# Attention scores on half the rows of TensorE, two heads in turn, and an instruction order ranked backward from the end

## The chip, the cores and the metric

The kernel runs on one core of a Trainium2 chip. A core has TensorE (PE in the profile; PEld is its weight loads), VectorE (DVE), ScalarE (ACT), GpSimd (POOL) and SyncE (SP), whose queue issues all of this kernel's DMAs. TensorE reads two operands of up to 128 rows from the on-chip memory and adds its products up in PSUM, which has eight banks of 512 columns. The metric is the device time of one launch in microseconds (us).

## What is computed

```python
scores = scale * np.matmul(q, k.transpose(0, 1, 3, 2))      # q, k, v: (4, 8, 576, 64)
thresh = np.max(scores, axis=-1, keepdims=True) - tau
scores = np.where(scores >= thresh, scores, -1000000000.0)
attn = np.exp(scores - np.max(scores, axis=-1, keepdims=True))
attn = attn / (np.sum(attn, axis=-1, keepdims=True) + 1e-09)
attn_out = np.matmul(attn, v)                               # -> x: (2304, 512)
x = (1 / (1 + np.exp(-(x @ w_gate))) * (x @ w_val)) @ w_out # first layer, d_ff 1536
out = (((x @ w1) * (x @ w2)) @ w3) @ w_out2                 # second layer, d_ff 1024
```

The inputs of the two layers come in double width and are turned into single width on the chip. Every product is made of three: an operand x is split into a high part and a low part (xh + xl), and high x low, low x high and high x high are added up in PSUM.

## The kernel before

**Attention.** The 4 batches of 8 heads are 16 pairs of heads. A pair's query and key are loaded (qm, km), turned on TensorE so that the 64 features of each of the two heads lie in rows (head 0 in rows 0 to 63, head 1 in 64 to 127), and split: xq and yq are the high and low parts of the scaled query, xk and yk those of the key. Each pair has nine slots: four blocks of 128 queries for each head, and one for the last 64 queries of both heads (qb holds them, with zeros in the other head's rows). A slot's scores (128 queries x 576 keys) are made by `s_mm` in two halves of 288 columns, into one of two PSUM tiles, `sbuf_[g % 2]`, for slot g (named ps_s). Then `s_max` on VectorE takes each row's maximum (L648), `s_exp` on ScalarE runs twice over the scores (L656, L657; the second writes e and the sum), `s_hi` and `s_lo` split e into two parts of half width (L668 or L666, L674), a DMA turns them (pt), and five slots later `pv` multiplies by the values (64-column matmuls into u). `x_norm`, `x_pe` and `x_act` normalise the pair's result and put it into XR (L732, L734).

**Two forms of the scores.** `ZP = 2 * NPAIR` makes the first eight pairs (pr < ZP) differ from the last eight. In the first eight, one head's query lies in qst[h] (named qa) and kst[h] (ka) with zeros in the other head's rows, so that a product over all 128 rows gives this head alone: three products, six matmuls a slot. In the last eight, `dup0` and `dup1` stack xq over yq and xk over xk by DMA, and `low0` and `low1` put yk over zeros (ylz): two products, four matmuls a slot, for ten DMAs a pair. Slots go through one head's four blocks, then the other's.

**Fillers.** Between slots, `fill` takes pieces of other work for TensorE: first `merge_gen` (w3 times w_out2, names ps, th, tl, woh, wol), then `l1_gen`, the first layer (ps_h, ps_o), three quarters of which lie beside the attention; its weights are cast on VectorE, ScalarE and GpSimd (w, t) and split (gh, vh, oh and gl, vl, ol). The last quarter, and the second layer (ps_ab, ps_y), come after the last pair.

**What sets the order.** Everything up to `cut`, the end of the attention, is put in order by the class `Plan`. It has a cost for each instruction, knows what must wait for what (`hard`: for the end of it; `soft`: for its begin only), and lays the instructions out engine by engine: of those ready, the one with the lowest rank goes next, and the rank is the place in the program. `pin` ties each engine's instructions to this order. What comes after `cut` is not planned.

Of the kernel before, what the change touches and what calls it, by code (L numbers as in the profile page):

```python
# [21 lines left out]
class Plan:  # L22
# [10 lines left out]
    SLACK = {"DMACopy": 3000.0, "DmaTransposeAnt": 1500.0}  # L33
    HOLD = 200.0

    def __init__(self, insts, cut, over, late=(), by=0):
# [137 lines left out]
    def time(self, n):  # L174
# [32 lines left out]
    def order(self):  # L207
# [100 lines left out]
def kernel(  # L308
# [22 lines left out]
    nc = tc.nc  # L331
# [15 lines left out]
    def mm(out_, lhsT, rhs, first, last):  # L347
        nc.tensor.matmul(out_, lhsT, rhs, start=first, stop=last)  # L348

# [41 lines left out]

    ZP = 2 * NPAIR
    qst = [[ap_.tile([P, NC * P], F32R, name=f"qa{h}_{i}") for i in range(2)] for h in range(2)]
    kst = [[ap_.tile([P, S], F32R, name=f"ka{h}_{i}") for i in range(2)] for h in range(2)]
# [3 lines left out]
    ylz = [ap_.tile([P, S], F32R, name=f"ylz_{h}") for h in range(2)]  # L398
    tails = ap_.tile([P, H, D], F32, name="tails")

    def attn_setup():
# [4 lines left out]
        for h in range(2):  # L406
            z = hsl[1 - h]
            nc.vector.tensor_copy(
                ylz[h][z].rearrange("p (a d) -> p a d", d=D),
                zf[z].rearrange("p (a d) -> p a d", a=1).to_broadcast([D, S // D, D]),  # L410
            )
        for h in range(2):
            z = hsl[1 - h]
            for t in (*qst[h], *(t[:, 0:NC * P] for t in kst[h])):
# [63 lines left out]
    def q_act(pr):  # L478
# [4 lines left out]
        nc.scalar.activation(xk[:, NM:S], pt[:, TL:2 * TL], AF.Copy)  # L483
        xq = ap_.tile([P, NM], F32R, tag="xq", name="xq", bufs=1)
        p.update(xq=xq, qb=qbd[pr % 2])
# [8 lines left out]
    def q_dve(pr):  # L494
# [6 lines left out]
        )  # L501
        yq = ap_.tile([P, NM], F32R, tag="yq", name="yq", bufs=1)
        p["yq"] = yq
# [10 lines left out]
        for sl in hsl:  # L514
# [3 lines left out]
            )  # L518

    def dup(pr, h):  # L520

        p = prep[pr]
        xq, yq, xk = (p[n].bitcast(F32) for n in ("xq", "yq", "xk"))
        if pr < ZP:
            return
        qa = qst[h][pr % 2]
        nc.sync.dma_start(qa[hsl[h]].bitcast(F32), xq[hsl[h]])
        nc.sync.dma_start(qa[hsl[1 - h]].bitcast(F32), yq[hsl[h]])
        ka = kst[h][pr % 2]
        for sl in hsl:  # L530
            nc.sync.dma_start(ka[sl].bitcast(F32), xk[hsl[h]])
        p.setdefault("qa", []).append(qa)
        p.setdefault("ka", []).append(ka)

    def low(pr, h):

        if pr < ZP:
            return
        nc.sync.dma_start(ylz[h][hsl[h]].bitcast(F32), prep[pr]["yk"][hsl[h]].bitcast(F32))

    def low0(pr):
        low(pr, 0)

    def low1(pr):
        low(pr, 1)

    def dup0(pr):
        dup(pr, 0)

    def dup1(pr):  # L550
        dup(pr, 1)

# [64 lines left out]

    def s_mm(g):
        pr, s = divmod(g, NSL)
        p = prep[pr]  # L620
        ps = sbuf_[g % 2][:, SO:SO + S]
        if s < 2 * NC:
            h, c = divmod(s, NC)
            cs = slice(c * P, (c + 1) * P)
            if pr < ZP:
                x, y = qst[h][pr % 2][:, cs], kst[h][pr % 2][:, cs]
                prods = [(x, p["xk"]), (y, p["xk"]), (x, p["yk"])]
            else:
                prods = [(p["qa"][h][:, cs], p["ka"][h]), (p["qa"][h][:, cs], ylz[h])]
        else:  # L630
            prods = [
                (p["qb"][:, 0, :], p["xk"]),
                (p["qb"][:, 1, :], p["xk"]),
                (p["qb"][:, 0, :], p["yk"]),
            ]
        for i, (a, r) in enumerate(prods):
            for j in range(2):
                mm(
                    ps[:, j * HS:(j + 1) * HS], a, r[:, j * HS:(j + 1) * HS],
                    i == 0, i == len(prods) - 1,  # L640
                )
        st[g] = {"ps": ps}

# [37 lines left out]
    def pv(g, g_at):  # L681
# [5 lines left out]
        if s < 2 * NC:  # L687
            h, c = divmod(s, NC)
            todo = [(h, p["u"][:, h, c, :])]
# [9 lines left out]
    def x_norm(pr):  # L699
# [436 lines left out]
    t_pe(0, 0)  # L1136
    for step in (q_pe, q_act, q_dve, k_pe, k_act, k_dve, dup0, low0, dup1, low1):
        step(0)
# [8 lines left out]
        3: ([k_act], [k_dve], [], [v_pe1], []),  # L1147
        4: ([], [v_scale], [dup0, low0, dup1, "k"], [], []),
# [3 lines left out]
        8: ([], [], [low1, "v"], [], []),  # L1152
    }
# [35 lines left out]
    for g in range(G + LAG + 3):  # L1189
# [313 lines left out]
```

## Time and profile before

| | |
|---|---|
| median of 3 runs | 1071.82 us (1071.23 to 1078.38) |
| the profiled execution | 1074.56 us, its span 1072.8 us |
| TensorE busy | 1004.5 us, 94% of the span |
| VectorE, ScalarE, GpSimd busy | 673.1, 663.7, 692.4 us |
| last of the attention into XR | 631.84 us |

The span is from the first to the last instruction; the 1.8 us beside it are not in the trace. A share of the whole span mixes stages with different limits, and TensorE's ends are modelled, so that its busy time says less than the distance from one matmul's start to the next one's.

### The profile page before, as it was taken

How to read it: one execution, taken by the hardware profiler on the slowest of the kernel's cores; microseconds unless marked ns; L12 is line 12 of the kernel's file. 1: busy time of each engine (PE TensorE's matmuls, PEld its weight loads, DVE VectorE, ACT ScalarE, POOL GpSimd, SP SyncE). 2: the span in 40 equal slices, each digit the busy share in tenths (PEclk: the TensorE clock that was granted, in tenths of full speed). 3: DMA queues.
4: the chain of work that ended last, by engine and by line, in shares of the span. 5: the costliest groups of instructions: out<-in, count | busy, mean ns of one | idle time of the engine just before them, and what ended most of it. 6: DMA issues, size and time to landing. Idle time of an engine off the chain costs nothing. (4 is left out here: it accounts for less than half of the span.)

```text
span 1072.8 us, 20181 instructions
## 1 busy us (share of the span) xinstructions
PE 1004.5 (94%) x7088; PEld 891.5 (83%) x7088; DVE 673.1 (63%) x1226; ACT 663.7 (62%) x1325; POOL 692.4 (65%) x587
## 2 busy tenths in 40 slices
PE   4599976899998999999999989999999999999997
PEld 3488865687887888888888879999999989989995
DVE  8896587777866655557554447776776725743741
ACT  6687699978879878879887664445432322422221
POOL 5966288899997777667766756767664723552530
PEclk9999969999999999999999999999999999999999
DMA  8899699999999999989987675767378619835822
GB/s 218 237 238 226 146 234 220 254 224 268 252 251 228 219 211 223 209 191 210 232 171 164 130 178 186 255 223 236 129 248 276 204 60 321 258 98 173 310 78 59
DMA packets 301844, 221.28 MB, mean 206 GB/s; under 512 B 221872, under 2 KB 250544, under 8 KB 301744
## 3 DMA queue, kind: packets, MB, share of 16 engines
q1 hardware_dynamic: 301744, 220.00, 80.9%
q8 instruction: 56, 0.92, 0.4%
q14 instruction: 44, 0.36, 0.1%
HBM read 133.17 MB, written 30.93 MB: 153 GB/s over the span
## 5 line engine op out<-in xcount | busy, mean ns | idle before, releaser
L674 POOL TENSOR_TENSOR h<-e,h 128x576 f16<-128x576 f32 x120 | 155.1, 1295 | 75.7 <-ACT h L668 43.0
L648 DVE TENSOR_SCALAR_CACHE_REDUCE e<-ps_s,tauc 128x576 f32<-128x576 f32 x144 | 117.1, 814 | 72.2 <-PE ps_s L348 31.9
L656 ACT ACTIVATE ps_s<-ps_s,nt 128x576 f32<-128x576 f32 x144 | 102.4, 712 | 50.0 <-DVE e L648 48.4
L657 ACT ACTIVATE e<-ps_s,ebias 128x576 f32<-128x576 f32 x144 | 106.5, 740 | 2.9 <-POOL vl L781 0.4
L348 PEld LDWEIGHTS <-pt 128*128 128x128 f16 x2240 | 76.7, 100 | 32.6 <-issue 23.1
L348 PE MATMUL ps_h<-xl,gh 128*128 128x512 f32 (+1 forms) x240 | 93.1, 388 | 3.9 <-POOL xl L781 2.8
L348 PE MATMUL ps_h<-xl,vh 128*128 128x512 f32 (+1 forms) x240 | 92.5, 385 | 0.0
L348 PE MATMUL ps_y<-wm,abh 128*128 128x512 f32 x288 | 91.4, 390 | 0.3 <-DVE wm L781 0.3
L348 PE MATMUL ps_o<-gvl,oh 128*128 128x512 f32 (+1 forms) x240 | 90.7, 378 | 0.0
L348 PE MATMUL ps_h<-xh,gh 128*128 128x512 f32 (+1 forms) x240 | 89.1, 371 | 0.0
L348 PE MATMUL ps_h<-xh,gl 128*128 128x512 f32 (+1 forms) x240 | 88.9, 371 | 0.0
L348 PE MATMUL ps_h<-xh,vh 128*128 128x512 f32 (+1 forms) x240 | 88.8, 370 | 0.0
L348 PE MATMUL ps_h<-xh,vl 128*128 128x512 f32 (+1 forms) x240 | 88.8, 370 | 0.0
L348 PE MATMUL ps_o<-gvh,ol 128*128 128x512 f32 (+1 forms) x240 | 88.5, 369 | 0.0
L348 PE MATMUL ps_o<-gvh,oh 128*128 128x512 f32 (+1 forms) x240 | 88.3, 369 | 0.0
L668 ACT ACTIVATE h<-e 128x576 f16<-128x576 f32 x126 | 86.0, 684 | 2.9 <-DMA pt<-h 1.5
L781 POOL TENSOR_TENSOR gl<-w,gh 128x512 fp32r<-128x512 f32 x42 | 55.0, 1310 | 49.3 <-ACT gh L780 48.7
L781 POOL TENSOR_TENSOR gvl<-gr,gvh 128x512 fp32r<-128x512 f32 (+1 forms) x48 | 60.3, 1256 | 10.2 <-ACT gvh L780 9.6
L780 ACT ACTIVATE abh<-r 128x384 fp32r<-128x384 f32 x48 | 24.2, 521 | 68.9 <-DVE r L1368 68.6
L781 POOL TENSOR_TENSOR ol<-w,oh 128x512 fp32r<-128x512 f32 x42 | 55.8, 1336 | 16.7 <-ACT oh L780 16.7
L781 POOL TENSOR_TENSOR vl<-w,vh 128x512 fp32r<-128x512 f32 x43 | 58.1, 1352 | 8.7 <-ACT vh L780 8.4
L348 PEld LDWEIGHTS ps_y<-wm,abh 128*128 128x128 f32 x288 | 54.0, 188 | 11.4 <-DVE wm L781 0.6
(208 smaller groups left out, 3021.0 us busy)
## 6 DMA issues: line engine op xcount, KB each, us to landing
wc<-sc_c SPq DMA_DIRECT2D x168, 256.0 KB, 3.4
w<-sc_w SPq DMA_DIRECT2D x35, 768.0 KB, 5.2
sc_c<-wc SPq DMA_DIRECT2D x56, 256.0 KB, 2.7
XR<-in_moe_w_out_dram SPq DMA_DIRECT2D x20, 512.0 KB, 4.9
sc_w<-w SPq DMA_DIRECT2D x11, 768.0 KB, 5.9
XR<-in_moe_w_dram SPq DMA_DIRECT2D x16, 512.0 KB, 4.7
raw<-in_moe_w_dram SPq DMA_DIRECT2D x16, 512.0 KB, 4.6
XR<-in_moe_w_gate_dram SPq DMA_DIRECT2D x12, 512.0 KB, 5.5
```

What stands on the lines that cost most here:

```text
L348: nc.tensor.matmul(out_, lhsT, rhs, start=first, stop=last)
L648: nc.vector.tensor_scalar(e, x["ps"], tauc, None, op0=ALU.add, op1=ALU.min, accum_out=nt)
L656: nc.scalar.activation(x["ps"], x["ps"], AF.Prelu, scale=-1.0, bias=x["nt"], alpha=STEEP)
L657: nc.scalar.activation(x["e"], x["ps"], AF.Exp, bias=ebias, accum_out=prep[pr]["sum"][:, s:s + 1])
L668: nc.scalar.activation(x["h16"][:, 0:S], x["e"], AF.Copy)
L674: eng.tensor_tensor(hb[:, S:2 * S], st[g]["e"], hb[:, 0:S], op=ALU.subtract)
L780: nc.scalar.activation(hi, x, AF.Copy)
L781: (lo_eng or nc.gpsimd).tensor_tensor(lo, x, hi.bitcast(F32), op=ALU.subtract)
```

## The change

The stacking DMAs and the zero-filled rows of the scores go (`ZP = 0 * NPAIR`; dup and low are gone, ylz too). Every pair's slots, but the ninth, take three products over the head's own 64 rows: head 0's operands lie in rows 0 to 63 of xq, yq, xk, yk, head 1's in rows 64 to 127. `s_mm` gets two slots at once, the two heads' slots of one block of queries, and writes their matmuls in turn, so that both PSUM tiles are filled together; slots now go block by block, head by head. xq and yq get two buffers each. The eight GpSimd copies of zeros into qst and kst stay.

`Plan` is told of each such row of matmuls (`beads`): within it a matmul waits only for the begin of the one ahead. It gets a cost for matmuls on 64 rows, and a new rank: `pin` runs `order` and `backward` twice, and `backward` lays the instructions out from the end, so that the rank becomes the order of the latest begins.

```diff
-    ZP = 2 * NPAIR
+    ZP = 0 * NPAIR
+    beads = []
...
-        xq = ap_.tile([P, NM], F32R, tag="xq", name="xq", bufs=1)
+        xq = ap_.tile([P, NM], F32R, tag="xq", name="xq", bufs=2)
...
-    def s_mm(g):
+    def s_mm(*gs):
+
+        todo = []
+        for g in gs:
+            pr, s = divmod(g, NSL)
+            p = prep[pr]
+            ps = sbuf_[g % 2][:, SO:SO + S]
+            c, h = divmod(s, 2)
+            cs = slice(c * P, (c + 1) * P)
...
+                sl = hsl[h]
+                xq, yq, xk, yk = p["xq"][sl, cs], p["yq"][sl, cs], p["xk"][sl], p["yk"][sl]
+            todo.append((ps, [(xq, xk), (yq, xk), (xq, yk)]))
+            st[g] = {"ps": ps}
+        row = []
+        for i in range(3):
+            for j in range(2):
+                js = slice(j * HS, (j + 1) * HS)
+                for ps, prods in reversed(todo):
+                    a, r = prods[i]
+                    mm(ps[:, js], a, r[:, js], i == 0, i == 2)
+                    row.append(len(nc.cur_bb.bb.instructions) - 1)
+        if len(gs) > 1:
+            beads.append(row)
...
+    def group(g):
+
         pr, s = divmod(g, NSL)
...
+        if pr < ZP or s == 2 * NC:
+            return [g]
+        return [] if s % 2 else [g, g + 1]
...
-    for step in (q_pe, q_act, q_dve, k_pe, k_act, k_dve, dup0, low0, dup1, low1):
+    for step in (q_pe, q_act, q_dve, k_pe, k_act, k_dve):
...
-            if g + 2 < G:
-                s_mm(g + 2)
             if g + 1 < G:
                 s_max(g + 1)
                 s_exp(g + 1)
+            if g + 2 < G and group(g + 2):
+                s_mm(*group(g + 2))
...
     def pin(self, tc):
+        for _ in range(self.ROUNDS):
+            self.order()
+            self.backward()
```

TensorE's order in pair 4 before: the two slots of a ps_s tile each, six matmuls a slot (x2 stands for the two halves), with other work between them.

```order
L348 MATMUL ps_s_91<-xk,qa_0_95 128x288 x2
L348 MATMUL ps_s_91<-xk,ka_0_99 128x288 x2
L348 MATMUL ps_s_91<-yk,qa_0_95 128x288 x2
L721 MATMUL ps_x<-ident,xn 128x128 x4
L348 MATMUL ps_h<-xl,gh 128x512
L348 MATMUL ps_h<-xh,gl 128x512
L348 MATMUL ps_h<-xh,gh 128x512
L348 MATMUL ps_s_92<-xk,qa_0_95 128x288 x2
L348 MATMUL ps_s_92<-xk,ka_0_99 128x288 x2
L348 MATMUL ps_s_92<-yk,qa_0_95 128x288 x2
```

After, in pair 4: one group, the two tiles in turn, with nothing between.

```order
L409 MATMUL ps_s_92<-xk,xq 128x288
L409 MATMUL ps_s_91<-xk,xq 128x288
L409 MATMUL ps_s_92<-xk,xq 128x288
L409 MATMUL ps_s_91<-xk,xq 128x288
L409 MATMUL ps_s_92<-xk,yq 128x288
L409 MATMUL ps_s_91<-xk,yq 128x288
L409 MATMUL ps_s_92<-xk,yq 128x288
L409 MATMUL ps_s_91<-xk,yq 128x288
L409 MATMUL ps_s_92<-yk,xq 128x288
L409 MATMUL ps_s_91<-yk,xq 128x288
L409 MATMUL ps_s_92<-yk,xq 128x288
L409 MATMUL ps_s_91<-yk,xq 128x288
```

The first of these now follows the last exponential of both tiles' earlier slots, where each tile's first matmul followed its own alone. In the last eight pairs TensorE's order before had four matmuls a slot, here between pieces of the first layer; in their place stands the same row of twelve a group.

```order
L348 MATMUL ps_h<-xh,vh 128x512
L348 MATMUL ps_s_92<-ka_0_97,qa_0_93 128x288 x2
L348 MATMUL ps_s_92<-ylz_106,qa_0_93 128x288 x2
L348 MATMUL ps_h<-xl,vh 128x512
```

ScalarE's order before, slots 58 and 59 (pair 6): the passes over the scores of the one tile and of the other, with other steps spread between.

```order
L656 ACTIVATE ps_s_91<-ps_s_91,nt 128x576
L657 ACTIVATE e,sum<-ps_s_91,ebias 128x576
L558 ACTIVATE xk<-ps_t 128x512
L780 ACTIVATE gh<-w 128x512
L668 ACTIVATE h_3598<-e 128x576
L767 ACTIVATE t_3625<-XR 128x512
L780 ACTIVATE gvh<-gr 128x512
L780 ACTIVATE vh<-w 128x512
L656 ACTIVATE ps_s_92<-ps_s_92,nt 128x576
L767 ACTIVATE t_3676<-XR 128x512
L657 ACTIVATE e,sum<-ps_s_92,ebias 128x576
```

After, the same slots, to the first pass of the next group.

```order
L689 ACTIVATE e,sum<-ps_s_91,ebias 128x576
L700 ACTIVATE h_3584<-e 128x576
L688 ACTIVATE ps_s_92<-ps_s_92,nt 128x576
L689 ACTIVATE e,sum<-ps_s_92,ebias 128x576
L812 ACTIVATE gvh<-gr 128x512
L1033 ACTIVATE th<-ps_h 128x512
L812 ACTIVATE gh<-w 128x512
L799 ACTIVATE t_3611<-XR 128x512
L700 ACTIVATE h_3675<-e 128x576
L614 ACTIVATE vb<-vs 128x128
L688 ACTIVATE ps_s_91<-ps_s_91,nt 128x576
```

The two slots' passes moved together, and six other steps now stand between the group's last and the next group's first.

## Rows read from the trace of the kernel before

**Rows 1.** Windows of L648, cut at pairs' first: busy us (count), clock, DMA share, GB/s.

```profile
59.80:100.90 41.10, 7.36 (x18) 1.00 1.08 232
...
321.20:632.00 310.80, 59.11 (x144) 0.99 0.93 198
```

**Rows 2.** Windows, the same cuts: busy us (count) of PE, PEld, DVE, ACT, POOL.

```profile
0.00:13.10 13.10, 5.13 (x20) 4.42 (x21) 10.09 (x22) 4.65 (x8) 6.11 (x18) 1.00 0.68 191
13.10:59.80 46.70, 26.45 (x150) 22.17 (x150) 41.40 (x78) 36.03 (x69) 39.98 (x33) 1.00 0.94 237
59.80:100.90 41.10, 40.76 (x339) 35.23 (x338) 32.52 (x65) 33.84 (x68) 25.24 (x23) 1.00 1.08 232
100.90:138.40 37.50, 34.02 (x340) 29.40 (x339) 19.26 (x42) 25.16 (x50) 12.02 (x10) 0.95 0.73 165
138.40:170.60 32.20, 21.94 (x218) 19.98 (x214) 26.61 (x54) 30.82 (x64) 28.56 (x25) 0.68 1.07 230
170.60:199.40 28.80, 22.51 (x238) 18.63 (x235) 20.41 (x46) 26.48 (x56) 25.07 (x21) 1.00 1.10 250
199.40:236.70 37.30, 33.62 (x251) 28.14 (x250) 27.84 (x56) 31.44 (x64) 33.94 (x29) 0.95 1.05 229
236.70:278.00 41.30, 40.11 (x328) 33.22 (x326) 32.25 (x63) 32.12 (x63) 38.55 (x32) 1.00 1.06 274
278.00:321.20 43.20, 43.20 (x339) 36.35 (x336) 29.57 (x61) 36.26 (x71) 41.14 (x34) 1.00 1.07 239
321.20:632.00 310.80, 305.29 (x2554) 251.65 (x2552) 174.17 (x353) 253.95 (x509) 217.17 (x174) 0.99 0.93 198
```

**Rows 3.** The chain that ended last, in order of time: start, length, what.

```profile
631.84 0.31 ACT XR L734
...
1033.03 32.65 PE ps_y L348 x144
```

**Rows 4.** TensorE's timeline in pair 7: start and length in us.

```profile
300.73 0.43 PE L348 MATMUL ps_s<-xk,qa 128*128 128x288 f32 x2
...
301.52 0.23 PE L348 MATMUL ps_s<-identb,vm 128*128 128x128 bf16 x1
...
301.79 0.47 PE L348 MATMUL ps_h<-xl,vh 128*128 128x512 f32 x1
302.11 0.39 PE L348 MATMUL ps_h<-xh,vl 128*128 128x512 f32 x1
302.34 0.40 PE L348 MATMUL ps_h<-xh,vh 128*128 128x512 f32 x1
```

**Rows 5.** TensorE's timeline in pair 12.

```profile
482.71 0.42 PE L348 MATMUL ps_s<-ka,qa 128*128 128x288 f32 x2
...
483.24 0.39 PE L348 MATMUL ps_h<-xl,vh 128*128 128x512 f32 x1
```

**Rows 6.** Groups by line and shape: busy us, mean ns, idle before them.

```profile
L348 PEld LDWEIGHTS <-pt 128*128 128x128 f16 x2240 | 76.7, 100 | 32.6 <-issue 23.1 <-DMA pt<-h 6.8 <-DMA km<-in_k_dram 0.5
L648 DVE TENSOR_SCALAR_CACHE_REDUCE e<-ps_s,tauc 128x576 f32<-128x576 f32 x144 | 117.1, 814 | 72.2 <-PE ps_s L348 31.9 <-PE ps_s L725 8.4 <-PE ps_s L473 8.1
L656 ACT ACTIVATE ps_s<-ps_s,nt 128x576 f32<-128x576 f32 x144 | 102.4, 712 | 50.0 <-DVE e L648 48.4
L657 ACT ACTIVATE e<-ps_s,ebias 128x576 f32<-128x576 f32 x144 | 106.5, 740 | 2.9 <-POOL vl L781 0.4
L348 PE MATMUL ps_s<-ylz,qa 128*128 128x288 f32 x128 | 27.7, 299 | 0.0
L488 ACT ACTIVATE qa<-ps_t,zq 64x512 fp32r<-64x512 f32 x16 | 10.9, 680 | 0.3
L490 ACT ACTIVATE xq<-ps_t,zq 128x512 fp32r<-128x512 f32 x8 | 5.6, 703 | 0.0
```

**Rows 7.** Waits in pairs 3 to 7 (138.4 to 321.2 us): total, times, longest.

```profile
ACT ps_s L656 <- DVE e L648: 13.4, 15, 1.8
...
PE ps_s L348 <- ACT e L657: 8.3, 7, 1.8
```

More of the change, by code (lines that the diff above doesn't have):

```diff
@@ L34, with __init__ @@
     HOLD = 200.0
-    def __init__(self, insts, cut, over, late=(), by=0):
+    ROUNDS = 2
+    def __init__(self, insts, cut, over, late=(), by=0, beads=()):
         self.later = [i for i in insts[cut:] if i.opcode in self.OPS]
@@ L48, in __init__ @@
         self.edges(over)
+        at = {i.name: n for n, i in enumerate(self.x)}
+        for row in beads:
+            row = [at[insts[i].name] for i in row]
+            for m, n in zip(row, row[1:]):
+                self.soft[n].add(m)
+                self.hard[n].discard(m)
+        ends = set()
+        for row in beads:
+            ends |= {at[insts[row[1]].name], at[insts[row[-1]].name]}
         behind = {insts[i].name for a, b in late for i in range(a, min(b, cut))}
@@ L51, in __init__ @@
         self.cost = [self.time(n) for n in range(len(self.x))]
+        for n in ends:
+            self.cost[n] = self.cost[n][0] + 100, *self.cost[n][1:]
     @staticmethod
@@ L187, in time @@
             h = self.size(ins[0]) == 2
+            if ins[0].ap[0][1] == 64 and k > 128:
+                side = ins[0].offset * self.size(ins[0]) // (ins[0].tensor.bytes() // 128) >= 64
+                return (4 if side else k / 2.4 + 11), 290, k / 2.4 * (0 if side else 1)
             iv = 29 if k <= 64 else 108 if f else 39 if h else k / 2.4 + 13
@@ L295, in order, with backward @@
         return seq
+    def backward(self):
+        N, E = len(self.x), ("PE", "DVE", "ACT", "POOL", "SP")
+        pred = [self.hard[n] | self.soft[n] for n in range(N)]
+        out = [0] * N
+        for n in range(N):
+            for q in pred[n]:
+                out[q] += 1
+        lat = [d - s for s, d in zip(self.start, self.done)]
+        held = [
+            c[0] if e in ("PE", "SP") else max(60, c[0] - self.OVER[e])
+            for c, e in zip(self.cost, self.e)
+        ]
+        ready, begin = [0.0] * N, [0.0] * N
+        avail = {e: [n for n in range(N) if not out[n] and self.e[n] == e] for e in E}
+        free = dict.fromkeys(E, 0.0)
+        for _ in range(N):
+            best = None
+            for e in E:
+                if not avail[e]:
+                    continue
+                n = min(avail[e], key=lambda n: (
+                    max(ready[n] + lat[n] - held[n] - free[e] - 1, 0), -self.done[n]
+                ))
+                s = max(free[e], ready[n] + lat[n] - held[n])
+                if best is None or s < best[0]:
+                    best = s, e, n
+            s, e, n = best
+            avail[e].remove(n)
+            begin[n] = free[e] = s + held[n]
+            for q in pred[n]:
+                out[q] -= 1
+                if q not in self.hard[n]:
+                    r = begin[n] - lat[q]
+                elif self.e[q] == self.e[n] != "SP":
+                    r = begin[n] - (lat[q] - 5 if e == "PE" else 0)
+                else:
+                    r = begin[n] + self.LAG[self.e[q]] + self.LEAD[e]
+                ready[q] = max(ready[q], r)
+                if not out[q]:
+                    avail[self.e[q]].append(q)
+        for i, n in enumerate(sorted(range(N), key=lambda n: -begin[n])):
+            self.rank[n] = i
     def pin(self, tc):
+        for _ in range(self.ROUNDS):
+            self.order()
+            self.backward()
         for e, l in self.order().items():
@@ L347, in mm @@
     def mm(out_, lhsT, rhs, first, last):
-        nc.tensor.matmul(out_, lhsT, rhs, start=first, stop=last)
+        return nc.tensor.matmul(out_, lhsT, rhs, start=first, stop=last)
     cst = ctx.enter_context(tc.tile_pool(name="cst", bufs=1))
@@ L390, in beside @@
         return sbuf_[g % 2][:, o:o + P]
-    ZP = 2 * NPAIR
+    ZP = 0 * NPAIR
+    beads = []
     qst = [[ap_.tile([P, NC * P], F32R, name=f"qa{h}_{i}") for i in range(2)] for h in range(2)]
-    kst = [[ap_.tile([P, S], F32R, name=f"ka{h}_{i}") for i in range(2)] for h in range(2)]
+    kst = [[ap_.tile([P, NC * P], F32R, name=f"ka{h}_{i}") for i in range(2)] for h in range(2)]
     qbd = [ap_.tile([P, 2, P], F32R, name=f"qbd_{i}") for i in range(2)]
@@ L397 @@
     vlt = [ap_.tile([P, 2, NKB, D], F16, name=f"vl_{i}") for i in range(2)]
-    ylz = [ap_.tile([P, S], F32R, name=f"ylz_{h}") for h in range(2)]
     tails = ap_.tile([P, H, D], F32, name="tails")
@@ L407, in attn_setup @@
             z = hsl[1 - h]
[L408 to L414, printed above, removed]
+            for t in (*qst[h], *kst[h]):
                 nc.gpsimd.tensor_copy(
@@ L501, in q_dve @@
         )
-        yq = ap_.tile([P, NM], F32R, tag="yq", name="yq", bufs=1)
+        yq = ap_.tile([P, NM], F32R, tag="yq", name="yq", bufs=2)
         p["yq"] = yq
@@ L518, in q_dve @@
             )
[L520 to L551, printed above, removed]
     def k_pe(pr):
@@ L616 @@
     NSL = 2 * NC + 1
-    def s_mm(g):
-        pr, s = divmod(g, NSL)
[L620 to L642, printed above, removed]
+    def s_mm(*gs):
[6 more added lines that the diff above has]
+            cs = slice(c * P, (c + 1) * P)
+            if s == 2 * NC:
+                xq, yq, xk, yk = p["qb"][:, 0, :], p["qb"][:, 1, :], p["xk"], p["yk"]
+            elif pr < ZP:
+                xq, yq, xk, yk = qst[h][pr % 2][:, cs], kst[h][pr % 2][:, cs], p["xk"], p["yk"]
+            else:
+                sl = hsl[h]
[13 more added lines that the diff above has]
+    def group(g):
+        pr, s = divmod(g, NSL)
+        if pr < ZP or s == 2 * NC:
+            return [g]
+        return [] if s % 2 else [g, g + 1]
     def s_max(g):
@@ L687, in pv @@
         if s < 2 * NC:
-            h, c = divmod(s, NC)
+            c, h = divmod(s, 2)
             todo = [(h, p["u"][:, h, c, :])]
@@ L707, in x_norm @@
             xn.rearrange("p c h d -> p h c d"), p["u"],
-            rs[:, 0:2 * NC].rearrange("p (h c x) -> p h c x", h=2, x=1).to_broadcast([P, 2, NC, D]),
+            rs[:, 0:2 * NC].rearrange("p (c h x) -> p h c x", h=2, x=1).to_broadcast([P, 2, NC, D]),
             op=ALU.mult,
@@ L1147 @@
         3: ([k_act], [k_dve], [], [v_pe1], []),
-        4: ([], [v_scale], [dup0, low0, dup1, "k"], [], []),
+        4: ([], [v_scale], ["k"], [], []),
         5: ([], [], [], [v_pe2], []),
@@ L1151 @@
         7: ([v_split], [], [], [], []),
-        8: ([], [], [low1, "v"], [], []),
+        8: ([], [], ["v"], [], []),
     }
@@ L1467 @@
             out_rows(g, t, pss[t])
-    Plan(nc.cur_bb.bb.instructions, cut, {"lp": ("mp",), "lb": ("mp",), "lx": ("mp",)}, late, BY).pin(tc)
+    Plan(nc.cur_bb.bb.instructions, cut, {"lp": ("mp",), "lb": ("mp",), "lx": ("mp",)}, late, BY, beads).pin(tc)
 _INS = [
```

## Prediction

> **What bounds the kernel now.** I read the table of windows first, cut at the first maximum (L648) of each pair of heads, since the engines' shares of the whole span hide the stages. Pair 0 begins at 13.1 us, pair 8 at 321.2; each window has 18 of L648, its nine slots with two instructions each (pair 1 stands for the others) [rows 1]. Then the engine that is nearest to full in each window [rows 2]. Pair 0 has VectorE and GpSimd at 41.4 and 40.0 of 46.7 us. Pair 1 has TensorE at 40.8 of 41.1, pair 2 at 34.0 of 37.5. Pairs 3 and 4 (138 to 199 us) belong to ScalarE, 30.8 of 32.2 and 26.5 of 28.8, with TensorE at 21.9 and 22.5. In pair 5 GpSimd (33.9 of 37.3) and TensorE (33.6) are level. In pairs 6 and 7 TensorE is full (40.1 of 41.3, 43.2 of 43.2) with GpSimd close behind (38.6, 41.1). In pairs 8 to 15 TensorE has 305.3 of 310.8 us and ScalarE only 254.0. The chain of work that ended last says the same of the rest: from 631.84 us, the last copy into XR, it is TensorE that the chain follows, with few other steps [rows 3]. That part, 441 us of 1072.8, is not touched by the change. So the change can act only before 632 us, and there in three ways: on TensorE where it is full, on ScalarE in pairs 3 and 4, and by the order everywhere.
>
> **The price of scores now.** In pairs 0 to 7 a slot has three products of two halves, six matmuls: 300.73 to 301.52 us, 0.79 us, 0.132 each [rows 4]. In pairs 8 to 15 it has four: 482.71 to 483.24, 0.53 us [rows 5]. The two heads' slots of one block of 128 queries (a group, from here on) so cost 1.58 us in the first eight pairs and 1.06 in the last eight. There are four groups in each pair of heads, and a ninth slot for the last 64 queries that the change leaves at six matmuls.
>
> **The price of scores after.** Twelve matmuls in a group, each on 64 rows, the heads in turn, as the order shows them. The step of 0.132 us is the same for the zero-filled products and the stacked ones, though half the rows of the former multiply zeros: it goes by the 288 columns, not by how many rows do useful work. No row of this trace has a matmul on 64 rows. If two of them, on different rows and into different banks, need not wait for each other, a group is six double steps, 0.79 us; if they do, it is twelve single ones, 1.58 us. I take the first end, because the step shows no price for rows. To this I add a price for going into and out of the half-row form: a 288-column matmul is shown for 0.30 us and the next begins after 0.132 [rows 6, 4], so 0.17 us passes between its last column and its end (ends are modelled). If the engine had to empty before it changes form, that is 0 to 0.34 us a group; I take one, 0.17, as the other should lie behind the group's own loads. A group is then 0.96 us, between 0.79 and 1.13. It saves 0.62 us in pairs 0 to 7 and 0.10 in pairs 8 to 15.
>
> The Trainium skill has a rule against the change here: TensorEngine Tiling (Array Packing), Key Properties, says that changing the tiling mode, not just the tile, drains TensorE. By it the group is the 1.13 us that the rows give for two drains, and pairs 8 to 15 lose 0.07 us a group; no run here has shown it yet.
>
> **Term by term, on the path.**
> - Pair 1: TensorE is full, 4 groups x 0.62 = 2.5 us.
> - Pairs 2 and 5: TensorE has nine tenths; I count half, 1.2 us each. In pair 5 GpSimd leaves 3.4 us.
> - Pairs 0, 3 and 4: TensorE waits there anyway; 0.
> - Pairs 6 and 7: 8 x 0.62 = 5.0 us, but GpSimd is next, and its idle time in the two windows is 2.7 + 2.1 = 4.8 us; so 4.8.
> - Pairs 8 to 15: 32 x 0.10 = 3.2 us; ScalarE, next, has 57 us free.
> - ScalarE: in pairs 0 to 7 the query is scaled and copied in two halves of 64 rows, 680 ns each, afterwards in one of 703 [rows 6]: 0.66 us a pair. VectorE's two steps become one likewise. Only ScalarE's, and only in pairs 3 and 4, ends last: 1.3 us.
> - Copies: ten stacking DMAs a pair, 80 in all, go from SP's queue. All fall in or just before pairs 8 to 15, where TensorE waited for a transposed tile (pt) for at most 6.8 us in the whole span, loads of weights included [rows 6]. That is the bound; I take 0, since TensorE is full there. VectorE's two copies of zeros into ylz leave the first 13 us, where it has 10.1 [rows 2]; 0, since pair 0's scores wait for the load of q too, and 3.0 us at most.
> - The new order: a bound above is the idle time of the fullest engine in each window before 321 us, 3.0 + 5.3 + 0.3 + 3.5 + 1.4 + 2.3 + 3.4 + 1.2 + 0 = 20 us. The bound below is the wait for both buffers, a rival. I take 0, since no row says which way a new order falls: TensorE has 552 matmuls of 512 columns ahead of pair 8's first scores in the order before and 542 now, so that the fillers stay in their stage.
>
> The sum is 2.5 + 2.4 + 4.8 + 3.2 + 1.3 = 14.2 us. The profiled execution took 1074.56 us (span 1072.8), so it would be 1060.4; it stood 2.7 us above the median of the three runs, 1071.82, from which the same saving gives **1058 us**. Without any drain the terms are 3.2, 3.2, 4.8 (GpSimd's cap), 8.6 and 1.3, together 21.1 us; with two they are 1.8, 1.8, 3.6, -2.2 and 1.3, together 6.3. The forecast's own range is 1051 to 1066.
>
> **Rival 1, slower: one ring in place of two.** Now each of the two score banks goes round alone: while one is under the maximum, ScalarE works on the other. Afterwards a group may begin only when both are free, so ScalarE's last exponential of a group, the twelve matmuls, and the maximum follow each other: 0.96 + 0.17 + 0.81 = 1.94 us in which ScalarE has no score work, four times a pair, 7.8 us; in pairs 3 to 7 it now waits 13.4 us for L648, 2.7 a pair [rows 7]. For it: in the same stretch TensorE's scores already wait 8.3 us for L657, so the release is what comes last. Against it: ScalarE has other work, in pair 3 its 30.8 us less nine times 0.71 + 0.74 [rows 6], or 17 us, and at the place shown the new order puts six other steps behind a group's second exponential. If the gap stays empty in pairs 3 to 7, 5 x 5.1 = 25.5 us are lost, and 1058 becomes 1084; from 56% of it on, the kernel is slower than before.
>
> **Rival 2: the weights come one after another.** Each matmul has a load of its own. The first 512-column matmul behind the 64-column ones keeps the next waiting for 0.32 us (301.79 to 302.11) in place of 0.23 [rows 4], so a load shows 0.09 us there, 0.12 with the step it hid behind. If two heads' loads go in turn, a double step is 0.18 to 0.24 us, a group 1.08 to 1.44; at 1.26 the 16 groups counted in pairs 1, 2 and 5 to 7 gain 5.1 us, pairs 8 to 15 lose 6.4, and with ScalarE's 1.3 nothing is left: 1072.
>
> The Trainium skill speaks against this rival: TensorE: Matmul & The Clock Gate, Part 3, The mechanism, has loads for another row group overlap the matmul in flight and such matmuls start some 4 ns apart. That would be the 0.79 us of the first end; the trace of before cannot show it.
>
> **Rival 3, slower: heads one after another.** Then the change doesn't do what it says on the chip: 1.58 to 1.75 us a group, pairs 8 to 15 lose 17 to 22 us, the others 0 to 2.7, ScalarE gives 1.3: 1087 to 1095. Against it is only that rows and banks differ.
>
> **Rival 4: the order fills idle time too.** If two thirds of the 20 us go as well, 1044.
>
> **How the numbers follow.** Chances: forecast 0.44, rival 1 0.12, rival 2 0.18, rival 3 0.08, rival 4 0.18. About 1% (10.7 us) is what a measurement of this kernel tells from no change. Faster by more, under 1061: two thirds of the forecast, rival 4, and a fifth of rival 2, together 0.52. Slower by more, over 1082.5: rival 3, the full price of rival 1 (0.07 of its 0.12), and a little of rival 2, 0.17. The rest, 0.31, is within 1%. For 8 in 10 the range leaves out the better half of rival 4 and what lies beyond rival 1's full price and rival 3's lower end: 1038 to 1086.
>
> **What would show it.** In the changed profile the two heads' score matmuls should start within a few ns of each other in twos, a group taking 0.8 to 1.1 us from its first start to the next row's; 0.18 to 0.24 us between twos means rival 2, 0.13 between single ones rival 3. The last copy into XR should come some 14 us before 631.84, with 441 us behind it as now. Rival 1 would show as ScalarE's idle time ahead of L688, put down to the maximum, growing by some us a pair in pairs 3 to 7 while their windows get longer. I am wrong if the windows of pairs 1, 6 and 7 don't shrink by 2 to 3 us each, or if those of 0, 3 and 4 change by more than a few us, which would be the order's doing.

## The result and the profile after

| | before | after |
|---|---|---|
| median of 13 runs each, taken together | 1072.44 us (1069.01 to 1078.38) | 1062.43 us (1059.12 to 1070.1) |
| ratio of the runs, 95% interval | | 0.9908, 0.9884 to 0.9933 |
| the profiled execution read here | 1074.56 us, span 1072.8 | 1063.45 us, span 1061.7 |
| last of the attention into XR begins | 631.84 us | 616.33 us |

The change gains 10 us, against 14 forecast: 1062.4 us, where 1058 was said. From here on a kernel's distance from before is its ratio less one, times 1071.8 us: the change is at -9.9 us (-12.4 to -7.2). The first profile of the changed kernel was its longest run, 1070.1 us; so a second one of the same kernel, near the median, is read here.

> The changed kernel as it is, for a second profile, since the first was of an execution 8 us over its median. If its long pairs 3 and 4 (36 and 39 us, the clock at half speed for 38 us) are the ring's doing, they stand here too; if they are that execution's, pairs 3 and 4 are nearer 32 us each and the span nearer 1060.

Pair 3 is 35.5 us long in both profiles. Pair 4 took 38.8 us in the first and takes 32.5 here, so its excess there was that execution's own.

Its windows, cut as in [rows 2] at the first maximum of each pair (L680 now): length, busy us (count) of PE, PEld, DVE, ACT, POOL, then the clock, DMA share and GB/s.

```profile
11.70:54.20 42.50, 24.87 (x171) 19.52 (x171) 36.86 (x75) 35.51 (x70) 38.24 (x32) 1.00 0.99 259
54.20:95.50 41.30, 39.85 (x338) 31.17 (x336) 32.27 (x65) 31.81 (x63) 26.52 (x22) 1.00 1.11 251
95.50:125.70 30.20, 29.14 (x317) 24.03 (x318) 18.67 (x42) 24.91 (x53) 14.86 (x15) 1.00 0.83 184
125.70:161.20 35.50, 21.24 (x225) 16.85 (x226) 29.28 (x58) 32.38 (x66) 33.22 (x27) 0.65 1.07 252
161.20:193.70 32.50, 27.22 (x255) 21.77 (x252) 21.69 (x48) 27.21 (x55) 25.44 (x22) 0.81 1.05 231
193.70:223.40 29.70, 29.38 (x241) 23.01 (x242) 26.83 (x53) 28.20 (x59) 28.90 (x25) 1.00 1.08 255
223.40:260.70 37.30, 36.64 (x353) 29.43 (x352) 28.39 (x58) 31.87 (x64) 35.06 (x30) 1.00 1.12 269
260.70:297.30 36.60, 35.85 (x273) 27.70 (x274) 28.49 (x57) 31.64 (x65) 33.80 (x27) 1.00 0.96 242
297.30:617.00 319.70, 312.35 (x2702) 244.56 (x2701) 182.48 (x354) 254.06 (x512) 228.22 (x181) 0.99 0.75 164
617.00:1061.70 444.70, 434.09 (x2340) 414.87 (x2340) 259.32 (x394) 152.31 (x310) 224.63 (x195) 0.99 0.59 193
```

Held against [rows 2], the pairs changed by -4.2, +0.2, -7.3, +3.3, +3.7, -7.6, -4.0 and -6.6 us. Pair 1, where TensorE was full, gained nothing; pairs 0 and 2 gained, where little was forecast; 3 and 4 became longer. In pair 3 TensorE is idle for 14.3 us in place of 10.3, its clock at 0.65 (0.68 before); in pair 4 it is idle for 5.3 us in place of 6.3 and busy for 27.2 in place of 22.5, its clock at 0.81 (1.00 before). Pair 8 begins 23.9 us sooner, but the last eight pairs then take 8.9 us more, and what follows 3.9 more. So the sum nearly fits the forecast, and its parts do not. TensorE's records before and in pair 8's stretch tell how much is only shifted: ahead of pair 8 there were 2196 matmuls before and are 2175 now; behind it 2554 and 2702, of which 8 x 16 = 128 are the two forms' difference, so some 20 have gone behind. Counted by form, the trace has 554 of the 512-column matmuls, which are fillers, ahead of pair 8 before and 543 now: 11 of them, at the 0.23 us from one to the next, are an estimated 2.5 us. So little of the 23.9 us is only shifted; for most of what the last eight pairs lose no cause was shown.

**The price of a group.** TensorE's timeline in pair 8: start and length in us.

```profile
304.15 0.40 PE L409 MATMUL ps_h<-xh,gh 128*128 128x512 f32 x1
304.48 0.53 PE L409 MATMUL ps_s<-xk,xq 64*128 64x288 f32 x4
304.85 0.42 PE L409 MATMUL ps_s<-xk,yq 64*128 64x288 f32 x4
305.11 0.43 PE L409 MATMUL ps_s<-yk,xq 64*128 64x288 f32 x4
305.47 0.33 PE L528 MATMUL ps_s<-ident,tails 128*128 128x128 f32 x1
```

Twelve matmuls take 304.48 to 305.47, 0.99 us, as in the median of the groups. By their starts in the trace the two heads' matmuls begin 4 ns apart or less (in other groups up to 15, but for four of 61, where one head lags by 0.09 us or more); the first two are followed after 0.24 us, the last after 0.23, the four steps between are 0.13. That is 6 x 0.13 and 0.11 us on entering, 0.09 on leaving the half-row form. The 512-column matmul ahead is left after 0.33 us (304.15 to 304.48) in place of 0.23: another 0.09 or 0.10. A group so costs TensorE some 1.08 us; it was 1.58 in pairs 0 to 7 and 1.06 in pairs 8 to 15.

**The waits in pairs 3 to 7** (125.7 to 297.3 us): total, times, longest.

```profile
PEld ps_s L409 <- ACT e L689: 12.9, 8, 4.2
ACT ps_s L688 <- DVE e L680: 10.8, 14, 2.7
PE ps_s L409 <- ACT e L689: 10.6, 6, 4.0
```

In [rows 7] ScalarE waited for the maximum for 13.4 us, and TensorE for the release of the score banks for 8.3 us with 1.8 the longest. ScalarE's wait has become less; TensorE's has grown a little, with pieces of up to 4.0 us.

**Groups by line and shape**, as in [rows 6].

```profile
L409 PEld LDWEIGHTS <-pt 128*128 128x128 f16 x2240 | 77.9, 101 | 38.4 <-issue 24.0 <-DMA pt<-h 13.0 <-DMA w<-sc_w 0.3
...
L545 ACT ACTIVATE xq<-ps_t,zq 128x512 fp32r<-128x512 f32 x16 | 10.9, 683 | 5.5 <-PE ps_t L518 5.3 <-PE ps_s L409 0.2
```

The query's scaling took 10.9 + 5.6 us before and 10.9 now, as priced. The wait for transposed tiles rose from 6.8 to 13.0 us, though 80 copies left the queue.

**The end of the attention**, in the chain that ended last, in order of time: start, length, what.

```profile
616.33 0.70 ACT XR L764
...
617.70 1.00 POOL xl L813
...
618.75 11.19 PE ps_h L409 x48
```

XR comes 15.5 us sooner. Then TensorE starts slowly: a window of 8 us from 617 has the granted clock at 0.57, where before 8 us from 632 had 1.00, and 384-column matmuls follow each other every 0.32 us until 624.35 and every 0.17 to 0.18 after. Seventeen steps at the lower level (1.2 of 2.4 GHz) cost some 2.6 us of the 3.9 that this stretch lost. The two windows, the change's first:

```profile
617.00:625.00 8.00, 6.25 (x21) 6.26 (x22) 4.88 (x4) 5.06 (x12) 4.84 (x4) 0.57 0.77 261
```

```profile
632.00:640.00 8.00, 6.12 (x35) 6.12 (x36) 4.93 (x4) 5.21 (x12) 4.88 (x4) 1.00 0.86 285
```

### The profile page after: what moved, and what is told of

Same layout as the page of the kernel before. It is cut to its first block, busy times and chain, and to the rows that moved or that the text cites. A ratio compares the mean times of both kernels' runs of the same rounds, so it can differ in the third digit from the quotient of the medians.

```text
span 1068.3 us, 20229 instructions
## 1 busy us (share of the span) xinstructions
PE 996.2 (93%) x7216; PEld 856.8 (80%) x7216; DVE 675.7 (63%) x1216; ACT 654.4 (61%) x1317; POOL 695.4 (65%) x587
## 4 chain that ended last, share of the span: by engine, by line
PE 78%; ACT 7%; DVE 5%; issue 3%; POOL 3%; DMA 2%; SPq 0%; DVEq 0%; ACTq 0%; POOLq 0%
PE ps_h L409 25%; PE ps_ab L409 16%; PE ps_o L409 13%; PE ps_y L409 8%; PE ps_s L409 8%; PE u L409 3%; PE ps L409 3%; ACT e L689 2%; ACT ps_s L688 2%; DVE e L680 1%; ACT h L700 1%; DVE rs L734 1%; PE ps_t L518 1%; PE ps L874 1%; POOL w L803 1%
## 5 line engine op out<-in xcount | busy, mean ns | idle before, releaser
L706 POOL TENSOR_TENSOR h<-e,h 128x576 f16<-128x576 f32 x120 | 157.7, 1319 | 84.6 <-ACT h L700 57.6
L680 DVE TENSOR_SCALAR_CACHE_REDUCE e<-ps_s,tauc 128x576 f32<-128x576 f32 x144 | 114.4, 814 | 66.3 <-PE ps_s L528 27.9
L688 ACT ACTIVATE ps_s<-ps_s,nt 128x576 f32<-128x576 f32 x144 | 101.9, 712 | 57.6 <-DVE e L680 56.9
L409 PEld LDWEIGHTS <-pt 128*128 128x128 f16 x2240 | 78.4, 101 | 36.9 <-issue 24.4
L813 POOL TENSOR_TENSOR vl<-w,vh 128x512 fp32r<-128x512 f32 x43 | 57.9, 1346 | 15.7 <-ACT vh L812 15.6
L409 PE MATMUL u<-vh,pt 128*128 128x64 f16 x640 | 60.0, 199 | 7.9 <-DMA pt<-h 7.5
L409 PEld LDWEIGHTS ps_y<-wm,abh 128*128 128x128 f32 x288 | 54.1, 188 | 12.9 <-DVE wm L813 2.1
```

The source lines that it names most:

```text
L409: return nc.tensor.matmul(out_, lhsT, rhs, start=first, stop=last)
L680: nc.vector.tensor_scalar(e, x["ps"], tauc, None, op0=ALU.add, op1=ALU.min, accum_out=nt)
L688: nc.scalar.activation(x["ps"], x["ps"], AF.Prelu, scale=-1.0, bias=x["nt"], alpha=STEEP)
L706: eng.tensor_tensor(hb[:, S:2 * S], st[g]["e"], hb[:, 0:S], op=ALU.subtract)
L813: (lo_eng or nc.gpsimd).tensor_tensor(lo, x, hi.bitcast(F32), op=ALU.subtract)
```

## The experiments

Two parts of the change were never apart in the prediction: the order that a new rank makes, and what the slots are. And the slots' change is two things: both banks are filled together, and the matmuls are on 64 rows. The theory behind the forecast is that the half rows give all of the gain; Rival 1 that the common release takes it back; Rival 4 that the order gives it.

**The new rank alone: newrank.** `backward` and the two rounds are put into the kernel before; slots and their forms stay.

```diff
     HOLD = 200.0
+    ROUNDS = 2
...
     def pin(self, tc):
+        for _ in range(self.ROUNDS):
+            self.order()
+            self.backward()
```

> The kernel before, its scores and copies untouched, with the rank by latest begins alone. Theory 1: within 4 us of before, 1068 to 1076. Theory 2: 1058 to 1065, the whole gain. Theory 3: in between or better, since it has no single ring to pay for.

Measured: 1063.8 us, ratio 0.9917 (0.9885 to 0.9950), -8.9 us. The order alone gives as much as the whole change. Two windows, from the start to pair 8 and from there to XR: first the kernel before, then newrank.

```profile
0.00:321.20 321.20, 267.74 (x2196) 227.54 (x2197) 239.96 (x479) 256.80 (x508) 250.60 (x219) 0.96 1.00 231
```

```profile
0.00:309.60 309.60, 266.98 (x2196) 225.48 (x2197) 243.39 (x479) 254.82 (x507) 244.99 (x213) 0.96 0.99 235
...
309.60:619.00 309.40, 305.37 (x2554) 251.47 (x2552) 176.93 (x353) 254.50 (x510) 225.58 (x180) 0.99 0.94 203
```

The same 2196 matmuls with the same busy time stand ahead of pair 8, and TensorE is idle for 42.6 us in place of 53.5. What the order gives is idle time of TensorE. Where it gives it, newrank's pairs 0, 2, 3, 4 and 5 to 7 show:

```profile
13.60:56.50 42.90, 27.17 (x150) 22.62 (x150) 39.09 (x73) 35.53 (x68) 38.07 (x32) 0.96 0.95 233
97.90:129.50 31.60, 31.39 (x325) 27.55 (x323) 18.59 (x42) 25.35 (x52) 12.41 (x10) 1.00 0.75 166
129.50:159.30 29.80, 21.40 (x210) 19.39 (x210) 25.79 (x55) 29.02 (x59) 27.02 (x24) 0.71 1.04 232
159.30:187.10 27.80, 22.90 (x241) 19.01 (x242) 23.39 (x48) 26.37 (x58) 23.83 (x20) 1.00 1.05 246
187.10:309.60 122.50, 118.02 (x910) 97.43 (x910) 94.85 (x177) 99.24 (x199) 109.75 (x90) 0.97 1.06 245
```

Pairs 0 and 2 are 3.8 and 5.9 us shorter than before by the order alone, nearly what they are in the change. Pairs 3 and 4 together are 3.4 us shorter, where the change made them 7.0 longer. Pairs 5 to 7 take 122.5 us, against 121.8 before and 103.6 in the change: that gain comes with the rest.

**The change without the new rank: oldrank.**

```diff
-    ROUNDS = 2
+    ROUNDS = 0
```

> The change with the rank by place in the program (no backward passes); scores on half rows, heads in turn, stay. Theory 1, the saved TensorE time carries the gain: a group still takes 0.99 us, time 1060 to 1066, about as the change (1062). Theory 2, the new rank carries it: 1070 or more. Theory 3, both matter and the half rows alone lose by their single ring: over 1075.

Measured: 1078.9 us, ratio 1.0066 (1.0043 to 1.0088), +7.1 us. With the rank by place in the program the new scores make the kernel slower. Over the whole attention TensorE waits for the release of the score banks longer than in any other kernel here:

```profile
PE ps_s L409 <- ACT e L689: 38.4, 17, 5.9
```

The same row before, in newrank and in the changed kernel:

```profile
PE ps_s L348 <- ACT e L657: 15.1, 11, 2.7
PE ps_s L395 <- ACT e L704: 12.3, 7, 4.7
PE ps_s L409 <- ACT e L689: 22.5, 13, 4.0
```

With the half-row scores in place the rank is worth 17 us (+7.1 to -9.9), nearly twice what it is alone.

**Both banks at once, on 128 rows: coupled.** newrank with two neighbouring slots as a group, their matmuls in turn, so that both banks must be free; products, rows and copies are those of before.

```diff
+    def group(g):
+        s = g % NSL
+        if s == 2 * NC:
+            return [g]
+        return [] if s % 2 else [g, g + 1]
...
         with tc.high_priority(offset=RING):
-            if g + 2 < G:
-                s_mm(g + 2)
             if g + 1 < G:
...
+            if g + 2 < G and group(g + 2):
+                s_mm(*group(g + 2))
```

> The kernel before with the new rank, its products over 128 rows kept, but two neighbouring slots' matmuls in turn, so that a group needs both score banks free; TensorE's time for scores is as in newrank (1063.8). Theory ring: what half rows save on TensorE is lost by waiting for both banks; then this kernel has the loss without the saving, 8 to 18 us over newrank, 1072 to 1082. Theory no ring: the saving lies where ScalarE and GpSimd set the time; then within 4 us of newrank.

Measured: 1083.91 us, ratio 1.0135 (1.0120 to 1.0149), +14.5 us: 23.4 us (some 4 either way) slower than newrank. This is Rival 1 by itself, and in sum near its full price of 25.5 us. Its two windows, its pairs 3 and 4 and its wait for the release, then the changed kernel ahead of pair 8.

```profile
0.00:326.70 326.70, 268.23 (x2202) 227.77 (x2203) 255.35 (x481) 256.52 (x512) 250.48 (x219) 0.93 0.94 228
326.70:639.10 312.40, 305.76 (x2548) 251.49 (x2546) 179.77 (x351) 249.76 (x506) 219.68 (x174) 0.99 0.91 196
...
132.90:175.50 42.60, 26.12 (x281) 23.72 (x279) 34.37 (x57) 34.75 (x69) 33.37 (x28) 0.76 0.99 241
175.50:209.80 34.30, 27.94 (x249) 23.91 (x250) 25.95 (x54) 29.51 (x59) 25.17 (x20) 0.90 0.86 212
...
PE ps_s L401 <- ACT e L725: 27.2, 8, 6.2
```

```profile
0.00:297.30 297.30, 248.66 (x2175) 196.95 (x2176) 228.90 (x469) 246.71 (x498) 242.21 (x211) 0.94 1.01 242
```

TensorE's busy time ahead of pair 8 is as in newrank (268 and 267 us); its idle time is 58.5 us in place of 42.6, and its wait for the release over the attention 27.2 us in place of 12.3. The price does not lie where Rival 1 had put it, all in pairs 3 to 7: the two profiles are 20.2 us apart, and of these pairs 3 and 4 have 19.3 (76.9 against 57.6 us, with 79 matmuls more in them), pairs 5 to 7 give 5.6 back (116.9 against 122.5), and the rest lies ahead of and behind these.

Between coupled and the changed kernel busy time ahead of pair 8 falls by 19.6 us and idle time by 9.9, and the runs by 24.4 us (some 3 either way). Of the 19.6 us, 13 fillers of 512 columns that have gone behind (556 and 543) are an estimated 3.0. The 24.4 us are what the 64-row form, with the copies and zero rows that it saves and its slots block by block, gives where both kernels fill both banks at once.

**One head after the other: headbyhead**, and **one slot at a time: singles.** In the first, a group's six matmuls of one head come first, then the other's; in the second a group is one slot besides. The planner's cost of a matmul is made to fit in both, but the 0.1 us that it counts at either end of a row goes with a group, so that the slots of singles have none in its sum.

```diff
-        for i in range(3):
-            for j in range(2):
-                js = slice(j * HS, (j + 1) * HS)
-                for ps, prods in reversed(todo):
+        for ps, prods in reversed(todo):
+            for i in range(3):
+                for j in range(2):
+                    js = slice(j * HS, (j + 1) * HS)
...
-        if pr < ZP or s == 2 * NC:
-            return [g]
-        return [] if s % 2 else [g, g + 1]
+        return [g]
```

> The change with a group's matmuls head after head in place of in turn (the planner is told of the longer row). If two heads' matmuls overlap only when they alternate, a group takes 1.6 to 1.8 us, and where TensorE is full (pairs 1, 2, 5 to 7 counted as 16 groups, pairs 8 to 15 as 32) 0.6 us a group or 29 us come on top: 1085 to 1095. If the chip overlaps them in any order: 1062. If TensorE is not what the time hangs on: 1062 to 1070 with groups of 1.6 us.

> As headbyhead, but each slot by itself, so that each score bank again goes round alone; 12 matmuls for two slots as there. If the single ring costs ScalarE time (rival 1, up to 25 us), it is 10 to 25 us faster than headbyhead. If not, within 4 us of it.

Measured: headbyhead 1093.12 us, ratio 1.0188 (1.0143 to 1.0233); singles 1121.27 us, 1.0452 (1.0412 to 1.0492). The first is 30 us slower than the change: turns are what makes half rows pay. The second was to gain from its two free rings, and is 28 us slower than the first. TensorE's timeline says why, first in headbyhead.

```profile
193.08 0.40 PE L409 MATMUL ps_h<-xh,gh 128*128 128x512 f32 x1
193.40 0.53 PE L409 MATMUL ps_s<-xk,xq 64*128 64x288 f32 x2
193.77 0.29 PE L409 MATMUL ps_s<-xk,yq 64*128 64x288 f32 x1
193.78 0.39 PE L409 MATMUL ps_s<-xk,xq 64*128 64x288 f32 x1
193.90 0.29 PE L409 MATMUL ps_s<-xk,yq 64*128 64x288 f32 x1
194.01 0.29 PE L409 MATMUL ps_s<-xk,xq 64*128 64x288 f32 x1
...
194.41 0.42 PE L409 MATMUL ps_s<-yk,xq 64*128 64x288 f32 x2
194.76 0.20 PE L409 MATMUL ps_s<-vh,pt 128*128 128x64 f16 x1
```

A third xk,xq, the other head's first matmul, starts at 193.78, 0.38 us into the group and with the first head's third (193.77), though it stands behind all six of that head in the order. So the twelve take 1.36 us (median 1.37 of 56 groups), neither 0.99 nor two times that. Then a slot in singles.

```profile
200.65 0.53 PE L409 MATMUL ps_s<-xk,xq 64*128 64x288 f32 x2
201.03 0.42 PE L409 MATMUL ps_s<-xk,yq 64*128 64x288 f32 x2
201.29 0.42 PE L409 MATMUL ps_s<-yk,xq 64*128 64x288 f32 x2
201.65 0.20 PE L409 MATMUL u<-vl,pt 128*128 128x64 f16 x1
```

Six matmuls alone take 0.99 us (median of 106 slots), as long as twelve in turn, and more than six on 128 rows, 0.79 [rows 4]: the price of entering and leaving is paid whole for each slot.

**The bank freed one pass sooner: early** (on the change) and **early_newrank** (on newrank). ScalarE's first pass writes its result to e, and the second reads it there, so that the bank is free after the first.

```diff
-        nc.scalar.activation(x["ps"], x["ps"], AF.Prelu, scale=-1.0, bias=x["nt"], alpha=STEEP)
+        nc.scalar.activation(x["e"], x["ps"], AF.Prelu, scale=-1.0, bias=x["nt"], alpha=STEEP)
         nc.scalar.activation(
-            x["e"], x["ps"], AF.Exp, bias=ebias, accum_out=prep[pr]["sum"][:, s:s + 1]
+            x["e"], x["e"], AF.Exp, bias=ebias, accum_out=prep[pr]["sum"][:, s:s + 1]
```

> The change, but ScalarE's first pass over the scores writes into e and the second reads e, so that a bank is free one pass (0.74 us) sooner. Theory ring: the ring of a group is shorter by 0.74 us or more, and 4 to 12 us come back: 1050 to 1058. Theory no ring: within 4 us of the change's 1062.

> The kernel before with the new rank and the same earlier release. Theory ring: with two rings there is little to give back, within 4 us of newrank (1064). Theory no ring: the same. If ScalarE's passes themselves get faster or slower by the other memory, this shows it: 1058 or 1070.

Measured: early 1064.55 us, ratio 0.9946 (0.9932 to 0.9961), 4.1 us slower than the change; early_newrank 1071.18 us, 1.0005 (0.9982 to 1.0028), 9.4 us slower than newrank. The edit brought a price of its own, in the groups by shape of early:

```profile
L689 ACT ACTIVATE e<-e,ebias 128x576 f32<-128x576 f32 x144 | 111.2, 774 | 1.2
L688 ACT ACTIVATE e<-ps_s,nt 128x576 f32<-128x576 f32 x144 | 105.9, 738 | 39.7 <-DVE e L680 38.5
```

With the bank in place of e the two passes took 740 and 712 ns [rows 6], so ScalarE has some 60 ns more for each of 144 slots, 8.6 us. TensorE's wait for the release fell from 22.5 to 15.7 us in early. The same edit costs 5.3 us less where one release frees both banks, but the intervals of four ratios add up to as much. So it points to the release and doesn't settle it.

**Half rows in the first eight pairs alone: hybrid**, and **in pairs 5 to 7 alone: mixed.** hybrid is the changed kernel with stacked copies and single slots in pairs 8 to 15, mixed has the zero rows of before in pairs 0 to 4 besides.

```diff
-        if pr < ZP or s == 2 * NC:
+        if pr >= HP or s == 2 * NC:
             return [g]
         return [] if s % 2 else [g, g + 1]
```

```diff
-    ZP = 0 * NPAIR
+    ZP = 5
```

> Half rows in pairs 0 to 7, the stacked copies and single slots of before in pairs 8 to 15, new rank. A half-row group takes 0.99 us and 0.09 more ahead of it, the stacked one 1.06, so TensorE's time in the last eight pairs is the same. Theory ring, there too: 1054 to 1060. If the ring costs nothing where TensorE is full: 1060 to 1065.

> New rank; zero-filled products and single slots in pairs 0 to 4, half rows in groups in pairs 5 to 7, stacked copies and single slots in pairs 8 to 15. If the ring costs where ScalarE is the fuller (pairs 3 and 4: 64 us in hybrid, 58 in newrank) and half rows pay where TensorE is (pairs 5 to 7: 107 and 122 us), it has both: 1045 to 1054. If what a stage gains only moves fillers there, as hybrid: 1056 to 1061.

Measured: hybrid 1058.45 us, ratio 0.9908 (0.9876 to 0.9940); mixed 1061.25 us, 0.9912 (0.9888 to 0.9936). hybrid is where the change is, so that the half rows neither gain nor lose in pairs 8 to 15 what can be measured here, some 4 us either way. mixed was to keep newrank's pairs 3 and 4 and the half rows' gain in 5 to 7, and is no faster than the change. One window, its pairs 5 to 7:

```profile
193.50:307.70 114.20, 109.84 (x916) 85.92 (x912) 90.71 (x174) 93.74 (x192) 105.63 (x86) 1.00 1.05 260
```

They take 114.2 us, against 122.5 in newrank (187.1 to 309.6) and 103.6 in the change; but they begin 6.4 us later than in newrank, though ahead of them every slot is as there. The planner lays the whole program out anew for each kernel, and why the gains don't add up is open.

**The rank in one part alone: rank_first and rank_rest.** newrank, where the instructions from pair 3 on (rank_first), or those ahead of it (rank_rest), keep the rank by place.

```diff
+        for n in range(N):
+            if (n < self.mark) != self.first:
+                self.rank[n] = n + (N if self.first else -N)
```

> The kernel before with the rank by latest begins for the instructions written ahead of pair 3 only; all later ones keep their place in the program and come behind. If the new order's gain of 9 us arises in pairs 0 to 2, as the traces' begins of pair 3 say (138.5 before, 129.5 in newrank), it is all here: 1060 to 1066, pair 3 beginning at 127 to 132. If it is spread, 1066 to 1072.

> The other half: the new rank from pair 3 on, the first three pairs by place in the program. If the gain arises in pairs 0 to 2: 1068 to 1075, pair 3 beginning at 136 to 141. If it is spread: 1063 to 1069.

Measured: 1067.01 us, ratio 0.9960 (0.9939 to 0.9981), and 1067.84 us, 0.9968 (0.9953 to 0.9984): -4.3 and -3.4 us, together -7.7 of the -8.9 of both. In rank_first pair 3 begins at 130.7 us, near newrank's 129.5 (138.4 before), but half of that is gone at the end. The order's gain is spread, not one move in one place.

## Why the prediction was right in its number and wrong in its steps

The time lies in the range and in the forecast's own (1051 to 1066). But the mechanism was another. Its sum was 14.2 us, 12.9 from the half rows on TensorE and 1.3 from ScalarE. Measured one after the other, the change is -8.9 by the order (newrank), +23.4 by the common release (coupled against newrank), -24.4 by the 64-row form and what it saves (the change against coupled): -9.9. That the number came out is luck: a gain that I put at nothing and a loss that I left to a rival met a gain of the form that is nearly twice my 12.9. The split depends on that path, since the order is worth 17 us with the half rows and 8.9 without.

- **The price of a group** (0.96 us, 0.79 to 1.13): 0.99 us and 0.09 ahead of it, 1.08, within the bounds. The term was mis-sized by 0.12 us, since three places pay and I counted one: entry, exit and the matmul ahead. The Trainium skill, TensorEngine Tiling (Array Packing), Key Properties, has a change of the tiling mode drain TensorE; the trace agrees, and singles shows it best, where half of the work takes the same 0.99 us.
- **Rivals 2 and 3 fell.** Starts of two heads' matmuls mostly 4 ns apart or less, double steps of 0.13 us: loads and matmuls of the two row groups go beside each other. The Trainium skill, TensorE: Matmul & The Clock Gate, Part 3, The mechanism, gives some 4 ns, and the trace agrees. Rival 3's times lay 29 to 37 us over the forecast; headbyhead, whose groups take 1.37 us where Rival 3 had 1.58 to 1.75, lies 30 over the change.
- **Pairs 1, 6 and 7** (2 to 3 us each): 0, 4 and 7 us. My own test of it fails on pair 1, which TensorE filled before: it has 338 matmuls (339 before) and 1.5 us of idle time in place of 0.3. And in pairs 6 and 7 GpSimd, whose idle time I took for a cap, has 68.9 us of work in place of 79.7; TensorE has 626 matmuls in place of 667. A cap from one stage doesn't bind where a planner moves the work between stages. Pairs 2 and 5 (1.2 us each) became 7.3 and 7.6 us shorter: 5.9 of the first the order gives alone, of the second nothing (38.2 us in newrank, 37.3 before).
- **Pairs 0, 3 and 4** (0): 4.2 us shorter, 3.3 and 3.7 longer. Pair 0 is the order's doing, as my sign for it said (newrank has 3.8 of it); pairs 3 and 4 are not that of the order by itself, which shortens them; coupled, with the common release, has them longer still.
- **Pairs 8 to 15** (3.2 us): no gain that hybrid can tell, to some 4 us either way. At 1.08 against 1.06 us a group none follows from the price.
- **ScalarE** (1.3 us) and **the copies** (0): ScalarE's scaling became 5.6 us less in sum, about as counted; how much of it reached the end was not tried alone. The wait for transposed tiles didn't fall with the copies, but rose by 6.2 us, in hybrid too, which keeps all 80 (13.1 us); newrank has 3.8 us, coupled 1.9, oldrank 6.3 and singles 1.6, so it comes with groups of half rows and the new rank together. Why is open.
- **The new order: "I take 0".** This is the step that failed. -8.9 us by itself, inside the bound of 20 us that I had worked out and then left to Rival 4. It removed 10.9 us of TensorE's idle time ahead of pair 8; the bound had added up something else, the idle time of the fullest engine in each window of [rows 2]. That no row says which way an order falls was true, but 0 was then no better founded than 10.
- **Rival 1** had its price nearly right in sum, 25.5 us foreseen and 23.4 measured, and was given 0.12. The place was right in part: between the profiles of coupled and newrank 13.7 of 20.2 us lie in pairs 3 to 7, all of it in 3 and 4. Against the rival stood that ScalarE has other work to fill the gap. It has: its wait for the maximum fell in pairs 3 to 7, from 13.4 to 10.8 us. But the gap is TensorE's too, which finds both banks taken and has nothing ready of the fillers, and I had said that it would show on ScalarE. It shows in TensorE's wait for the release over the attention: 15.1 us before, 12.3 in newrank, 27.2 in coupled, 22.5 in the change.
- **The half rows' own gain** is larger than the 12.9 us of the sum. In a common ring the matmuls of a group stand between ScalarE's last exponential and the next maximum, in every pair and not only where TensorE is full: 32 groups x (1.58 - 1.08) are 16 us in pairs 0 to 7. The busy time ahead of pair 8 fits it, 19.6 us less than in coupled of which some 3.0 are fillers gone behind; why all of it reaches the end is argued, not shown, and 8 us of the 24.4 stay open.

## What to carry to other kernels

When one change holds a new form and a new order, price the order as a term of its own: here it was worth 8.9 us alone and 17 with the rest, and a version with each part alone tells it in two runs. Where two buffers are to be filled together, two rings become one, and the wait can fall on the engine that fills them: here TensorE waited 14.9 us more and the kernel took 23 us more, nearly all that half-row products gave. Products on 64 rows pay when two row groups take turns in one row, since a row of six matmuls for one head took as long here as a row of twelve for two.

## What the runs showed of the hardware

- Going from 128-row to 64-row matmuls and back cost 0.28 us or so for a row of them, whether six or twelve, in three places: 0.09 us ahead, 0.11 on entry, 0.09 on exit.
- Without turns, TensorE still began the other row group's matmuls early: in headbyhead the second head started with the first's third matmul, ahead of three that stand before it in the order, and a group took 1.37 us.
- A ScalarE pass over 576 columns took longer with e, which lies in the on-chip memory, in place of PSUM as its output (712 to 738 ns) or as its input (740 to 774 ns). The Trainium skill, ScalarE: Activation LUTs, Step-by-step: what each stage is for, calls PSUM the faster destination; the trace agrees, and shows the same for the source.
